# Complex products by three real ones, the overlap of one spectrum on VectorE, and a new order of stores and table transfers, in a long convolution with a gated state space model

## The chip, the cores and the metric

The kernel runs on one core of a Trainium2 chip. The metric is the device time of one execution in microseconds (us). The core's engines each work through a queue of their own in order and wait for one another by semaphores: TensorE (PE) multiplies matrices into PSUM, VectorE (DVE) and ScalarE (ACT) work elementwise, GpSimd (POOL) here mostly issues transfers that add into their destination, and SyncE (SP) issues the plain and the transposing transfers.

## What is computed

Two layers are mixed by a gate. Layer A is a diagonal state space model over 2048 steps with 1024 channels and 1024 complex states. Layer B multiplies a short convolution of k (4 taps) by v and convolves the product along the sequence with a filter as long as the sequence itself.

```python
g = sigmoid((x * gate_w).sum(-1, keepdims=True))
# layer A
B_bar = ((Lam_bar - 1.0) / Lam)[:, None] * Bmat
Bu = einsum("bld,pd->blp", x + 0j, B_bar)
for t in range(L):
    h = Lam_bar[None, :] * h + Bu[:, t, :]
y = 2.0 * einsum("blp,dp->bld", hseq, Cmat).real + x * Dskip
# layer B (q is x)
kv = k_shift * v
y = irfft2(rfft2(kv_pad) * rfft2(kf_pad))[:, :S]
y = x * (y + kv * ssm_D)
# out
g * a + (1 - g) * b
```

All inputs and the output are bfloat16; x, k and v have 2048 rows of 1024 columns.

## The kernel before, in words

**Layer B by blocks.** The 1024 channels are taken in eight groups of 128 (c = 0 to 7). The sequence is cut into four blocks of 512. Filter and signal of a block are folded and multiplied by cosine and sine tables on PE: `fwd_K` (line 636) forms the filter's spectrum in four tiles `psk`, `fwd_V` (line 674) the signal's in four tiles `psv`. ACT copies them from PSUM to `KH[c]` (kept in the buffers `BT` 2 and 3 by turns) and `VH[c]` (tiles `Vh`). Each holds two parts (c = 0 cosine, 1 sine), four blocks and 512 frequencies: 4096 columns.

The filter's block b overlaps block b - 1. For all groups but the last, `fwd_K` has PE add this part: eight more matmuls of 384 columns in each pair of tiles (lines 647 to 649). For group 7 DVE does it afterwards (`overlap_K`, line 667).

`products` (line 687) multiplies the spectra: a complex product for each pair of blocks (a, b) with a + b under 4, summed by the output block. It does so with four real products for a complex one. `A` in `acc` collects them; `wkh` and `t` hold parts. One addition of 3072 columns (from `n1`, in `wkh`) is not done by DVE but by an adding transfer that POOL issues (`gather`, line 717). The last four operations combine the parts and write the inverse's input back into `Vh` (`whole[c]`). `inverse` (line 769) multiplies it by inverse tables on PE (two tiles `psz`), ACT copies the tiles to `cv`, and SP stores them to scratch memory `cv_scr` (line 782).

Ahead of the spectra, `taps` (line 573) makes the short convolution on PE, `times_v` (line 603) multiplies by v on DVE and mirrors the result (`mirror` on PE, `lo` on ACT, `ev` on DVE, an adding transfer into `ks`). `fold_columns`, `fold_K` and `mirror_K` fold the filter. `spread` makes shifted copies of `kT` and `kB` for `taps`.

**Layer A in the gaps.** `Bu` (line 835) multiplies x by B in 16 pairs of tiles, odd and even rows apart. For the first two groups `Bu_tile` (line 867) runs in three steps: 16 matmuls into a tile `odd`, 16 into `even`, and four with a diagonal of lambda that close `even`. For the next two `Bu_halves` (line 892) has two such products of 16 and an empty step. `parts` (line 1187) is a generator over the 24 steps of these four; the main loop steps through it to put the products between the work of layer B. `turn_table` (line 471) builds a table of angles: ACT writes `hr`, a transfer adds its halves, and ACT takes sines in the next iteration.

**The order** is written by hand. `put` (line 93) makes each instruction follow the one before it on its engine, so an engine's queue is the order in which the Python code calls it; nearly every instruction therefore carries line 95 in the profile. The main loop (line 1190) runs c = 0 to 6. Iteration c runs the inverse of c - 1, the products of c, the spectra of c + 1 and the folding and taps of c + 2. All PSUM tiles come from one pool of four. After the loop come the products and inverse of group 7, the rest of Bu, the scans on DVE and the output product with C on PE (tiles `psy`).

## Time and profile before

| | |
|---|---|
| median of three runs | 382.45 us (378.86 to 383.15) |
| the profiled execution | 381.19 us, its span 379.4 us |
| granted TensorE clock | 0.998 of full speed |
| instructions in the span | 6680 |
| ACT busy | 303.6 us, 80% of the span |
| POOL busy | 78.0 us, 21% |
| bytes moved by transfers | 70.99 MB, mean 187 GB/s |
| `acc<-wkh`, 768 KB each, six times | median 8.3 us from issue to landing |
| `cv_scr<-cv`, 256 KB each, 16 times | median 3.7 us |
| `hr<-hr`, 256 KB each, four times | median 6.4 us |

A row of the timeline gives the start of an instruction or of several merged ones, their length, the engine, the operation with the tile it writes and the tiles it reads (out<-in), its shape, and a count. In square brackets stands how long the engine was idle ahead of it and who released it. In the answer on waits a row reads: engine and tile, who it waited for, microseconds in all, times, the longest. In the chain of work that ended last each row is a stretch of the path from the first to the last instruction, with the engine that held it. Matmuls overlap, and their ends are modelled: one of 512 columns is listed with 379 ns, while their starts are 216 ns apart.

### The profile page before, as it was taken

Reading aid. Unit: us, or ns where it says so; the run is one execution under the profiler, and the core shown is the slowest. Engines: PE = TensorE matmul, PEld = TensorE weight load, DVE = VectorE, ACT = ScalarE, POOL = GpSimd, SP = SyncE. Lnnn points to the kernel's source line nnn. Section 1 sums busy time; section 2 is a strip of 40 time slices with the busy share of each in tenths; the row PEclk is TensorE's granted clock in tenths of the full one; section 3 lists DMA queues with packets and bytes.
Section 4 is the critical chain, followed back from the end, with each engine's and each line's share of the span. In section 5 each row is a group of like instructions: output and inputs, shape, how many; then the busy total and the mean of one; then the engine's idle time right before and its main releaser. Section 6 shows DMA issues by size and latency. Waiting matters only on the chain.

```text
span 379.4 us, 6680 instructions
## 1 busy us (share of the span) xinstructions
PE 373.6 (98%) x2469; PEld 202.4 (53%) x2469; DVE 368.0 (97%) x596; ACT 303.6 (80%) x465; POOL 78.0 (21%) x106
## 2 busy tenths in 40 slices
PE   8999999999999999999999999999999999999996
PEld 5666457566584756754454444444445444444444
DVE  8899999999999999999999999999999999999984
ACT  5779998998989999777999699977979968936301
POOL 4011020020301102022012014122426322532000
PEclk9999999999999999999999999999999999999999
DMA  7879999999999998999999999946999998997223
GB/s 168 162 117 232 209 210 209 226 214 212 223 191 193 214 192 177 187 208 151 188 209 226 228 199 246 211 70 119 185 248 157 268 248 178 189 244 125 57 83 111
DMA packets 125827, 70.99 MB, mean 187 GB/s; under 512 B 104601, under 2 KB 107553, under 8 KB 125794
## 3 DMA queue, kind: packets, MB, share of 16 engines
q1 hardware_dynamic: 112416, 45.90, 55.4%
q0 software_dynamic: 12256, 24.38, 37.8%
q10 hardware_dynamic: 1122, 0.28, 0.4%
q8 instruction: 19, 0.31, 0.3%
q14 instruction: 14, 0.11, 0.1%
HBM read 15.48 MB, written 8.39 MB: 63 GB/s over the span
## 4 chain that ended last, share of the span: by engine, by line
PE 91%; DMA 6%; ACT 2%; SPq 0%; issue 0%; DVE 0%; ACTq 0%
PE psy L95 29%; PE both L95 22%; PE psk L95 10%; PE taps L95 6%; PE psv L95 6%; PE psz L95 5%; PE even L95 4%; PE odd L95 3%; DMA kT<-in_B_k_dram 3%; PE foldk L95 3%; DMA kT<-kT 2%; DMA kB<-kT 1%; ACT Vh L95 1%; PE p L95 1%; PE mirror L95 1%; ACT hr L95 1%
## 5 line engine op out<-in xcount | busy, mean ns | idle before, releaser
L95 PE MATMUL psy<-CT,U 128*128 128x512 bf16 (+1 forms) x426 | 93.2, 374 | 0.0
L95 PEld LDWEIGHTS <-U 128*128 128x128 bf16 x492 | 48.1, 98 | 55.6 <-issue 0.3
L95 PEld LDWEIGHTS <-BT 128*128 128x128 bf16 x544 | 50.5, 98 | 33.5 <-issue 0.2
L95 DVE TENSOR_TENSOR wkh<-BT,Vh 128x2048 bf16<-128x2048 bf16 (+3 forms) x31 | 44.7, 1460 | 0.0
L95 POOL DMA_DIRECT2D U<-Q x26 | 27.1, 1053 | 82.8 <-ACT Q L95 24.8
L95 DVE TENSOR_TENSOR acc<-BT,Vh 128x4096 bf16<-128x4096 bf16 (+3 forms) x19 | 37.0, 1950 | 0.6 <-ACT Vh L95 0.6
L95 ACT ACTIVATE Q<-U,lam 128x512 bf16<-128x512 bf16 (+1 forms) x60 | 35.0, 626 | 2.6 <-issue 1.9
L95 PE MATMUL both<-xT,BT 128*128 128x512 bf16 x160 | 35.3, 379 | 0.0
L95 ACT ACTIVATE Vh<-psv 128x1024 bf16<-128x1024 f32 x32 | 30.7, 1032 | 5.6 <-PE psv L95 5.6
L95 DVE TENSOR_TENSOR_SCAN A<-rv,init,A 128x256 bf16<-128x256 f32 x48 | 34.4, 736 | 0.0
L95 DVE TENSOR_TENSOR acc<-acc,wkh 128x1024 bf16<-128x1024 bf16 (+4 forms) x30 | 32.7, 1130 | 0.1
L95 ACT ACTIVATE BT<-psk 128x1024 bf16<-128x1024 f32 x31 | 30.1, 1037 | 2.3 <-PE psk L95 2.2
L95 ACT ACTIVATE U<-both 128x512 bf16<-128x512 f32 x44 | 24.3, 594 | 8.1 <-PE both L95 7.8
L95 POOL DMA_DIRECT2D acc<-wkh x8 | 9.8, 1219 | 100.2 <-DVE wkh L95 100.2
L95 PE MATMUL psk<-eok,SF 128*128 128x384 bf16 (+1 forms) x120 | 28.5, 354 | 0.0
L95 PEld LDWEIGHTS <-SF 128*128 128x128 bf16 x184 | 18.0, 98 | 18.8
L95 ACT ACTIVATE BT<-psy,gcols 128x1024 bf16<-128x1024 f32 (+1 forms) x6 | 6.3, 1043 | 24.7 <-issue 14.0
L95 PE MATMUL taps<-dg,kT 128*128 128x128 bf16 (+1 forms) x352 | 23.3, 219 | 1.0 <-DMA kT<-kT 0.5
L95 PE MATMUL psz<-Vh,CI 128*128 128x512 bf16 x64 | 24.3, 379 | 0.0
L95 PE MATMUL psz<-Vh,SI 128*128 128x512 bf16 x64 | 24.3, 379 | 0.0
L95 PEld LDWEIGHTS <-kT 128*128 128x128 bf16 x352 | 22.8, 104 | 2.7 <-DMA kT<-in_B_k_dram 1.4
L95 DVE TENSOR_TENSOR U<-U,trn 128x512 bf16<-128x512 bf16 (+1 forms) x60 | 22.0, 391 | 0.1
(225 smaller groups left out, 784.0 us busy)
## 6 DMA issues: line engine op xcount, KB each, us to landing
U<-Q POOLq DMA_DIRECT2D x26, 256.0 KB, 5.2
acc<-wkh POOLq DMA_DIRECT2D x6, 768.0 KB, 8.3
cv_scr<-cv SPq DMA_DIRECT2D x16, 256.0 KB, 3.7
kn<-in_B_ssm_k_dram SPq DMA_DIRECT2D x5, 512.0 KB, 4.4
v<-in_B_v_dram SPq DMA_DIRECT2D x5, 512.0 KB, 5.0
out_dram<-m SPq DMA_DIRECT2D x8, 256.0 KB, 4.6
BT<-cv_scr SPq DMA_DIRECT2D x7, 256.0 KB, 7.2
out_dram<-BT SPq DMA_DIRECT2D x7, 256.0 KB, 2.0
```

What stands on the lines that cost most here:

```text
L95: i = f(*a, **kw)
```

## The change

- Groups 1 to 7 get a `products` of their own with three real products for a complex one. DVE first forms the sum and the difference of the signal's two parts (`Vp`), and the sum of the filter's two parts (`S`, by the new `sum_K`); `pair` multiplies both filter parts by `Vp`, `one` multiplies `S` by the signal's first part. Group 0 keeps the old form as `products_0`.
- The adding transfer now adds both parts of `both` (3072 columns, as before), ahead of fewer operations of DVE. For group 7 DVE still does this addition itself.
- `apart_K = (3, NC - 1)`: spectrum 3 loses its overlap matmuls as spectrum 7 had done. `overlap_K` writes the overlapped blocks to a place in `wkh` (`K_later`) with two operations of 1536 columns.
- The steps of B are dealt out by a table, `count`; group (2, 0) runs its four products tile by tile, odd before even. There are 20 steps, since the empty ones are gone.
- For the inverses of c = 1 to 4, the stores of `cv` are issued only behind the load of v (`store_cv`).
- `turn_table`'s transfer is issued right after ACT's part, ahead of that of the products.
- `mirror_K` yields before its second copy, and with spectrum 3 the diagonals and the column fold for the next group come later in ACT's queue.

```diff
+    apart_K = (3, NC - 1)
+    K_later = {}
@@ mirror_K
         act(lo, ps, func=ACT.Copy)
+        yield
         act(eo[:, 1], kb[:, 2:4], func=ACT.Copy)
-        yield
@@ fwd_K
-                    mm(ps[:, cc], tab[:, mt, fsl], eo[:, cc, mt], mt == 0, c == NC - 1 and mt == 1)
-                for mt in range(0 if c == NC - 1 else 2):
+                    mm(ps[:, cc], tab[:, mt, fsl], eo[:, cc, mt], mt == 0, c in apart_K and mt == 1)
+                for mt in range(0 if c in apart_K else 2):
@@ overlap_K
-        for b in (3, 2, 1):
-            tt(K[:, 0, b], K[:, 0, b], K[:, 1, b - 1], ALU.add)
-            tt(K[:, 1, b], K[:, 1, b], K[:, 0, b - 1], ALU.subtract)
+        t = K_later[c] = WK[:, 4096:7168].rearrange("p (c b x) -> p c b x", c=2, b=3)
+        tt(t[:, 0], K[:, 0, 1:], K[:, 1, 0:3], ALU.add)
+        tt(t[:, 1], K[:, 1, 1:], K[:, 0, 0:3], ALU.subtract)
+
+    def sum_K(c):
+        S = sums[:, 1, 2048:].rearrange("p (b x) -> p b x", b=4)
+        if c in K_later:
+            tt(S[:, 0], K[:, 0, 0], K[:, 1, 0], ALU.add)
+            tt(S[:, 1:], K_later[c][:, 0], K_later[c][:, 1], ALU.add)
+        else:
+            tt(S, K[:, 0], K[:, 1], ALU.add)
@@ products, groups 1 to 7
+        def pair(o, b, n):
+            tt(o, bc(Kb(b), [128, 2, n, w]), Vp[:, :, 0:n], ALU.mult)
+        def one(o, b, n):
+            tt(o, bc(S[:, b:b + 1], [128, n, w]), V0[:, 0:n], ALU.mult)
+        tt(Vp[:, 1], Vt[:, 1], Vt[:, 0], ALU.add)
+        tt(Vp[:, 0], Vt[:, 1], Vt[:, 0], ALU.subtract)
+        yield
+        pair(both, 0, 4)
+        yield
+        pair(n1, 1, 3)
+        if by_dma:
+            gather(both[:, :, 1:], n1)
+        yield
...
+        pair(n3, 3, 1)
+        one(third, 0, 4)
+        yield
+        one(m1, 1, 3)
+        one(m3, 3, 1)
+        if not by_dma:
+            tt(both[:, :, 1:], both[:, :, 1:], n1, ALU.add)
+        one(m2, 2, 2)
+        tt(third[:, 1:], third[:, 1:], m1, ALU.add)
+        yield
+        pair(n2, 2, 2)
+        tt(m2[:, 1:], m2[:, 1:], m3, ALU.add)
+        tt(n2[:, :, 1:], n2[:, :, 1:], n3, ALU.add)
+        tt(third[:, 2:], third[:, 2:], m2, ALU.add)
+        yield
+        tt(both[:, :, 2:], both[:, :, 2:], n2, ALU.add)
+        yield
+        if c + 1 < NC and c + 1 not in apart_K:
+            sum_K(c + 1)
+        tt(both[:, 1], third, both[:, 1], ALU.subtract)
+        tt(both[:, 0], third, both[:, 0], ALU.add)
+        if c + 1 in apart_K:
+            sum_K(c + 1)
...
         tt(to[:, 0], lo, hi, ALU.subtract)
         tt(to[:, 1], lo, hi, ALU.add)
@@ inverse
-            move(cv_scr[c, :, 2 * par:2 * par + 2], cv)
+            stores.append((cv_scr[c, :, 2 * par:2 * par + 2], cv))
+            if c == 0 or c >= 5:
+                store_cv()
@@ main
-    parts = (None for i in range(4) for b in Bu(i) for _ in b)
+    def in_parts():
+        for i in range(4):
+            for b in ([tile_ for pair_ in [Bu(2)] for _ in range(2) for tile_ in pair_] if i == 2 else Bu(i)):
+                for _ in range(1 if i == 2 else 3 if i < 2 else 2):
+                    step(b)
+                    yield
+    count = {1: "D1 F1 G2", 2: "A1 B1 C1 D1 E2 F1", 3: "D2 F1", 4: "C1 D1 F1", 5: "D1 F2"}
...
+        if c == 1:
+            sum_K(1)
         step(old)
-        step(tabs)
+        steps(tabs, 2)
         run(back)
         step(tv)
-        steps(prod, 4)
+        steps(prod, 3)
...
             elif c < 5:
                 load("v", nn, True)
+                store_cv()
+            at("D")
             taps(nn, dg)
+            at("E")
             if c == 5:
                 load("v", nn)
+                store_cv()
...
         run(fk)
+        step(prod)
+        if n in apart_K:
+            overlap_K(n)
         run(prod)
-        if n == NC - 1:
-            overlap_K(n)
```

The letters of `count` are places in an iteration: A ahead of the first two tiles of `fwd_K`, B between its halves, C behind it, D ahead of `taps`, E behind it, F behind the first step of `times_v`, G between the halves of `fwd_V`; the number is how many steps run there. Before, the steps stood at D and F in nearly every iteration, at G in c = 1 and 3, and at other places in c = 2, 4, 5 and 6.

156 lines of the change are left out of this document (78 added, 78 removed).

## The prediction

> **What bounds the kernel now.** I read the page first: which engine is full, and what carries the chain that ended last.
>
> ```profile
> span 379.4 us, 6680 instructions
> PE 373.6 (98%) x2469; PEld 202.4 (53%) x2469; DVE 368.0 (97%) x596; ACT 303.6 (80%) x465; POOL 78.0 (21%) x106
> PE 91%; DMA 6%; ACT 2%; SPq 0%; issue 0%; DVE 0%; ACTq 0%
> ```
>
> TensorE (PE) is busy 98% of the span and VectorE (DVE) 97%. A busy PE need not run at its peak, so I asked next for PE's waits and then for the chain in order of time.
>
> ```profile
> PE taps L95 <- DMA kT<-kT: 0.5, 1, 0.5
> PE taps L95 <- DMA kT<-in_B_k_dram: 0.5, 1, 0.5
> ```
> ```profile
> 86.72 1.75 PE even L95 x16
> ...
> 142.31 6.05 PE psk L95 x32
> ...
> 165.25 3.45 PE psk L95 x16
> ```
>
> These are all of PE's waits after its first microsecond. The chain's rows (start, length, engine, tile, count) give PE's prices: one product of B, 16 matmuls, takes 1.75 us; a spectrum of K with its 16 overlap matmuls takes 6.05 us, the last one, which has none, 3.45. PE's starts follow each other at this pace from 59.5 us to the end, so PE's queue sets the time. DVE has hardly an idle stretch either: what it delivers to PE comes just in time, and any microsecond added to it can turn into a wait of PE. I judge the change by both: how much work leaves PE, and where PE then reaches something that another engine hasn't finished.
>
> **PE's work.** Spectrum 3 loses its 16 overlap matmuls: 6.05 - 3.45 = **2.60 us off**. The products of B are only moved. Counting the steps, whole products (odd or even) per iteration c = 1 to 6 go from 3, 3, 3, 3, 3, 1 to 3, 5, 2, 3, 3, 0. So PE's clock against before is +2 x 1.75 - 2.60 = +0.90 us at the end of c = 2, then -1.75 more in c = 3 and -1.75 in what lies ahead of the inverse of c = 5.
>
> **DVE's work**, from the timeline of one product stage (c = 4), and two other places for short operations:
>
> ```profile
> 116.86 2.29 DVE L95 TENSOR_TENSOR acc<-BT,Vh 128x4096 bf16<-128x4096 bf16 x1 [0.34 <-ACT Vh L95]
> 119.07 1.75 DVE L95 TENSOR_TENSOR wkh<-BT,Vh 128x3072 bf16<-128x3072 bf16 x1
> 120.73 2.29 DVE L95 TENSOR_TENSOR acc<-BT,Vh 128x4096 bf16<-128x4096 bf16 x1
> ...
> 124.61 0.69 DVE L95 TENSOR_TENSOR ev<-ks,lo 128x1024 bf16<-128x1024 bf16 x1
> 125.21 1.75 DVE L95 TENSOR_TENSOR acc<-acc,wkh 128x3072 bf16<-128x3072 bf16 x1
> ...
> 128.01 2.35 DVE L95 TENSOR_TENSOR wkh<-BT,Vh 128x2048 bf16<-128x2048 bf16 x2
> 130.28 1.29 DVE L95 TENSOR_TENSOR wkh<-wkh,t 128x1024 bf16<-128x1024 bf16 x2
> ...
> 133.83 2.35 DVE L95 TENSOR_TENSOR acc<-acc 128x2048 bf16<-128x2048 bf16 x2
> 136.21 2.36 DVE L95 TENSOR_TENSOR Vh<-acc 128x2048 bf16<-128x2048 bf16 x2
> ```
> ```profile
> 32.55 0.95 DVE L95 TENSOR_TENSOR wkh<-BT,Vh 128x1536 bf16<-128x1536 bf16 x1
> 33.42 0.69 DVE L95 TENSOR_TENSOR acc<-acc,t 128x1024 bf16<-128x1024 bf16 x1
> ```
> ```profile
> 185.68 2.35 DVE L95 TENSOR_TENSOR BT<-BT 128x512 bf16<-128x512 bf16 x6
> 187.94 4.42 DVE L95 TENSOR_TENSOR acc<-BT,Vh 128x8192 bf16<-128x8192 bf16 x1
> ```
>
> Neighbours overlap, so I price from start to start: 4096 elements 2.21 us, 3072 1.66, 2048 1.135 (half of 2.27), 1536 0.87, 1024 0.60, 512 about 0.38 (2.26 over six). An operation that needs the result of the one straight before it adds 0.11 (133.83 to 136.21 is 2.38 for a pair, not 2.27).
>
> The old stage takes 116.86 to 136.21 = 19.35 us up to the inverse's input `Vh`. The new one has eight of 2048 (9.08), one of 4096 (2.21), one of 3072 (1.66), two of 1536 (1.74), five of 1024 (3.00, `ev` among them), two of 512 (0.76) and three such neighbours (0.33): 18.78. So three real products are worth only 0.57 us a stage: fewer elements, but 21 operations for 18. The Trainium skill ("VectorE: DVE Perf Modes", section "The DRAIN you can't avoid") speaks against this shape: the pipe empties after every operation, so their number should be kept small. The rows' own price of one more operation is 2 x 1.135 - 2.21 = 0.06 us, and it is in the sum already.
>
> Around it: c = 1 forms its own K sum first (+1.135, net +0.57). c = 2 takes on the overlap of spectrum 3 (two of 1536, 1.74) and splits its sum (+0.1): net +1.27. c = 6 has the same ahead of its `Vh` (+1.27), where six operations (2.26) stood behind it. c = 7 saves about 1.7, since it adds 3072 elements where it added 6144, and forms no further sum. In all DVE saves some 2.8 us, but is late by 0.57 + 1.27 = 1.84 us at the end of c = 2. From c = 7 on it is ahead, so the scans cost PE nothing.
>
> **Where PE waits instead.** First a held PSUM tile. The last `even` tile of group (1, 1) now opens at the end of c = 2 and is closed in c = 3, so iteration 3 starts with three rotating PSUM tiles, not four. PE's first spectrum tile must wait for ScalarE's (ACT's) first `cv`; before, it was the second.
>
> ```profile
> 96.08 0.59 PE L95 MATMUL psk<-eok,CF 128*128 128x512 bf16 x2
> ...
> 97.27 0.49 PE L95 MATMUL psk<-eok,NCF 128*128 128x384 bf16 x2
> 97.82 0.59 PE L95 MATMUL psk<-eok,CF 128*128 128x512 bf16 x2
> ```
> ```profile
> 93.48 0.66 ACT L95 ACTIVATE hr<-hr 128x512 f32<-128x512 f32 x1
> ...
> 96.73 1.95 ACT L95 ACTIVATE cv<-psz 128x1024 bf16<-128x1024 f32 x2
> ...
> 135.88 3.77 ACT L95 ACTIVATE Vh<-psv 128x1024 bf16<-128x1024 f32 x4 [0.27 <-PE psv L95]
> ```
>
> Before, PE lost only 0.23 us here (97.27 to 97.82 for two matmuls of 0.16). Now PE comes to that point at 96.08 + 0.90 = 96.98. ACT empties four `Vh` tiles in a row (as at 135.88), which moves its table work from 93.48 to about 94.35 and frees the first `cv` at 97.82 + 0.87 = 98.69. That is a wait of 1.71, **1.48 more** than before. Its bounds are -0.23 (ACT early) and 1.71. PE's clock after c = 3 is then +0.90 + 1.48 - 1.75 = +0.63.
>
> Second, DVE against the inverse of c = 5 and c = 6, and of c = 1:
>
> ```profile
> 66.46 2.36 DVE L95 TENSOR_TENSOR Vh<-acc 128x2048 bf16<-128x2048 bf16 x2
> ...
> 159.64 2.36 DVE L95 TENSOR_TENSOR Vh<-acc 128x2048 bf16<-128x2048 bf16 x2
> ...
> 183.41 2.36 DVE L95 TENSOR_TENSOR Vh<-acc 128x2048 bf16<-128x2048 bf16 x2
> ```
> ```profile
> 68.76 0.38 PE L95 MATMUL psz<-Vh,CI 128*128 128x512 bf16 x1
> ...
> 161.21 0.38 PE L95 MATMUL psz<-Vh,CI 128*128 128x512 bf16 x1
> ...
> 186.61 0.38 PE L95 MATMUL psz<-Vh,CI 128*128 128x512 bf16 x1
> ```
>
> The first half of `Vh` is done 1.22 us after its start, at 160.86 for c = 5. The stage starts when ACT has emptied PE's `psv`, so with PE: 160.86 + 0.63 - 0.57 = 160.92. PE now wants it at 161.21 + 0.63 - 1.75 = 160.09. **PE waits 0.83.** From 0 (DVE quicker by that much) to 1.5 if the bubbles between short operations are twice mine. At c = 6 `Vh` is ready at 184.63 + 0.06 + 1.27 = 185.96, PE comes at 186.61 - 0.29 = 186.32: no wait.
>
> At c = 1 PE lost 0.73 us waiting for `kT<-kT` (0.5 of it in the row above; the rest is the modelled end of its last matmul). The table's transfer now goes before the large gather, and the gather itself starts later, so `kT<-kT` has less beside it. But `Vh` of c = 1 is ready at 66.46 + 1.22 + 0.57 = 68.25 where PE would come at 68.76 - 0.73 = 68.03: at most 0.51 is won, at least 0. I take **0.4 off**, since only a small wait for the gather stands against it.
>
> The gather is the unknown:
>
> ```profile
> 49.31 1.75 DVE L95 TENSOR_TENSOR wkh<-BT,Vh 128x3072 bf16<-128x3072 bf16 x1
> ```
> ```profile
> 51.36 1.20 POOL L95 DMA_DIRECT2D acc<-wkh  x1 [14.69 <-DVE wkh L95]
> ```
> ```profile
> acc<-wkh POOLq DMA_DIRECT2D x1, 768.0 KB, 9.4
> ```
> ```profile
> acc<-wkh POOLq DMA_DIRECT2D x1, 768.0 KB, 6.5
> ```
> ```profile
> DMA to landing us min/median/max: 6.1/8.0/9.4
> ```
>
> GpSimd (POOL) issues it 2.05 us after the start of DVE's operation that fills `n1`. From `ev` to the operation that needs it lie 7.8 us of DVE work by the prices above, after the 1.66 of `n1`: DVE is there 7.4 us after the issue, where by the same prices it used to come 11.5 us after it. The same transfer took 9.4 us beside two stores of `cv` and a `kT<-kT` (c = 2), and 6.5 in c = 6, where the stores were over sooner. Moving those stores behind `v`, some 10 us later, empties its neighbourhood in c = 2 to 5, so I take 7.4 or less: no wait. The stores themselves sit in SyncE's (SP's) queue ahead of the `kT` load, which is held for ACT anyway, so they cost nothing there unless they slow `v`. The Trainium skill ("DMA: Bandwidth & Descriptors", section "Anatomy of one DMA — SWDGE (gpsimd) path") gives 2.0 us plus bytes over 436 GB/s, an estimate of 3.8 us here. By that the gather never matters and the sum stays as it is; the rows above stand at 6.5 to 9.4, so the trace disagrees and the rows decide.
>
> The remaining edits are free: `mirror_K`'s copy moves behind ACT's other work in c = 5, and its result is used ten microseconds later (PE's 165.25). The later fold of spectrum 4 leaves ACT's queue for the earlier K tiles.
>
> **The sum.** -2.60 + 1.48 + 0.83 - 0.40 = -0.69 us. The profiled execution took 381.19 us with 1.8 around its span, and the runs shown have a median of 382.45 (378.86 to 383.15). From 381.19 I get **380.5 us**.
>
> **Rivals.** (1) PE's floor: ACT and DVE are early enough, so the held tile and the inverses cost nothing and both old waits go: 381.19 - 2.60 - 0.73 - 0.23 = **377.6**. For it: each wait I add is under 2 us and hangs on differences of a few tenths. Against it: both come from work that is counted, not guessed. (2) The gather lands late, the mechanism that ends slower: if it keeps its old landing times, 9.4 where I quoted it and near 8 to 9.4 elsewhere, c = 1 to 5 lose about 1.9, 2.0, 0.5, 0.7 and 1.1, in all 6.2 us on DVE. `Vh` of c = 5 comes at 160.86 + 0.57 + 1.27 - 3 x 0.57 - 0.34 (the wait on ACT that it swallows) + 6.2 = 166.85, PE's inverse starts 5.6 us later than before, and nothing gives that back: **386.8**. It decides from landings of about 7.5 us on: 0.7 us in all of such waits uses up the gain. For it: nearly all landings of before lie above that. Against it: the neighbours that made them long are moved. (3) The deferred stores meet `v` and `kT` on the DMA queues, and `taps` of the next iteration waits as at 59.5 us, 0.5 to 0.7 in three iterations: about **382**.
>
> **Numbers.** My forecast 0.45, (1) 0.28, (2) 0.19, (3) 0.08. About 1% is what a measurement of this kernel can tell from no change. The range runs from 377.2, just under (1), to 384.8, which holds a half-late gather; what lies beyond is the upper half of (2) and little else. Faster by over 1% takes a time under about 377.5 to 378.6, depending on which of the runs is the base: most of (1), 0.24. Slower by over 1%: the larger part of (2), 0.17. Within 1%: 0.59.
>
> **What would show it.** PE's chain should show spectrum 3 at 3.45 us. A gap of PE before the first `psk` near 97 to 99 us, released by ACT's `cv`, confirms the held tile; its absence speaks for (1). A PE gap before `psz` near 160 us, released by DVE, confirms the second. DVE's busy time should come out near 365 us. A DVE wait on `acc`'s DMA ahead of the last addition, repeated in c = 1 to 5, would make me wrong toward (2), and landings of `acc` say by how much. If `taps` waits for `kT` or `kB` in several iterations, it is (3).

## The result, and the profile after

The changed kernel is slower: 385.49 us in the median of 20 runs (382.61 to 398.0) against 380.17 for the kernel before (378.86 to 392.48, also 20). The ratio is 1.0111 with an interval of 1.0075 to 1.0146; like all ratios below it is formed without the executions that are several us slower at a lower clock. The forecast was 380.5, with a range up to 384.8. Each kernel has one profile, of a single execution. The experiments are read mainly from where things stand in these profiles, and the ratios are beside them.

The page of the changed kernel (span, busy time of the engines, and the chain that ended last by engine):

```profile
span 380.8 us, 6658 instructions
PE 370.1 (97%) x2453; PEld 199.4 (52%) x2453; DVE 365.3 (96%) x620; ACT 303.5 (80%) x465; POOL 76.6 (20%) x106
PE 78%; issue 10%; DMA 6%; DVE 2%; ACT 2%; POOL 1%; POOLq 0%; DVEq 0%; ACTq 0%
```

PE and DVE both do less than before (373.6 and 368.0), and yet the span is longer. So something waits. The answer on PE's waits (us in all, times, the longest) has four rows after the start:

```profile
PE psv L95 <- DMA ks<-lo: 2.4, 1, 2.4
PE psk L95 <- ACT cv L95: 1.5, 1, 1.5
...
PE odd L95 <- DMA xT<-in_A_x_dram: 1.1, 1, 1.1
PE psz L95 <- DVE Vh L95: 0.7, 1, 0.7
```

The second and the fourth were forecast (1.71 and 0.83). The first and the third were not. To place them, here are PE's rows from the timeline: the first inverse matmul of c = 0, c = 1 and c = 6 (`psz`), and the four waits.

```profile
43.18 0.39 PE L95 MATMUL psz<-Vh,CI 128*128 128x512 bf16 x1
...
56.50 1.91 PE L95 MATMUL odd<-xT,BT 128*128 128x256 bf16 x16 [1.14 <-DMA xT<-in_A_x_dram]
...
64.90 0.59 PE L95 MATMUL psv<-ks,SF 128*128 128x512 bf16 x2 [2.44 <-DMA ks<-lo]
...
70.10 0.38 PE L95 MATMUL psz<-Vh,CI 128*128 128x512 bf16 x1
...
99.99 0.59 PE L95 MATMUL psk<-eok,CF 128*128 128x512 bf16 x2 [1.52 <-ACT cv L95]
...
162.51 0.39 PE L95 MATMUL psz<-Vh,CI 128*128 128x512 bf16 x1 [0.69 <-DVE Vh L95]
...
187.93 0.38 PE L95 MATMUL psz<-Vh,CI 128*128 128x512 bf16 x1
```

The same mark for c = 0 in the kernel before (those of c = 1 and c = 6, 68.76 and 186.61, stand in the prediction), and the first `psv` that reads `ks` there, which doesn't wait:

```profile
45.00 0.39 PE L95 MATMUL psz<-Vh,CI 128*128 128x512 bf16 x1
...
63.55 0.59 PE L95 MATMUL psv<-ks,SF 128*128 128x512 bf16 x2
```

These marks cut the comparison into stretches that don't depend on the start, which was 1.82 us quicker in this execution of the changed kernel (43.18 for 45.00) although the code up to there is nearly the same, and varied between 43.1 and 45.9 over all the kernels below.

| from psz to psz | before | after | difference |
|---|---|---|---|
| c = 0 to c = 1 | 23.76 | 26.92 | **+3.16** |
| c = 1 to c = 6 | 117.85 | 117.83 | -0.02 |

Behind the mark of c = 6 the two spans differ by nothing: 379.4 - 186.61 = 192.8 and 380.8 - 187.93 = 192.9. **In these two profiles all of the loss lies in iteration 1.**

That last stretch is not always so short. Of the 19 profiles of this document ten have 192.7 to 194.3 us there and nine 196.5 to 206.3, among them the kernel before with one edit (experiment 4). In all nine PE waits 2.5 to 2.8 us for ACT's `U` ahead of a `psy`, and ACT has waited 4.3 to 13.5 us for loads between 225 and 262 us; in the ten others ACT waits 2.5 or less. In the last kernel of the table below (timelines of ACT and of PE):

```profile
243.51 1.15 ACT L95 ACTIVATE pbb<-pbb,omg 128x1024 bf16<-128x1024 bf16 x1 [5.57 <-DMA pbb<-cv_scr]
```
```profile
256.87 1.02 PE L95 MATMUL psy<-CTa,U 128*128 128x512 bf16 x4 [2.83 <-ACT U L95]
```

So a profiled time can be some 4 us or more longer for a reason that lies behind the loop. How often this happens to each kernel is not known, with one profile of each.

In iteration 1 POOL issues in another order. Before, and after (timeline of POOL):

```profile
55.84 0.91 POOL L95 DMA_DIRECT2D ks<-lo  x1 [3.28 <-DVE ev L95]
56.41 1.22 POOL L95 DMA_DIRECT2D hr<-hr  x1
```
```profile
46.20 0.89 POOL L95 DMA_DIRECT2D hr<-hr  x1 [11.35 <-ACT hr L95]
53.07 1.21 POOL L95 DMA_DIRECT2D acc<-wkh  x1 [5.99 <-DVE wkh L95]
53.78 1.43 POOL L95 DMA_DIRECT2D ks<-lo  x1
```

The transfers of iteration 1 and their landing in us, in the changed kernel:

```profile
hr<-hr POOLq DMA_DIRECT2D x1, 256.0 KB, 9.2
```
```profile
acc<-wkh POOLq DMA_DIRECT2D x1, 768.0 KB, 9.2
```
```profile
ks<-lo POOLq DMA_DIRECT2D x1, 256.0 KB, 11.1
```

Before, the gather left at 51.36 and `ks` 4.5 us behind it; `ks` landed in 7.1, at 62.9, just ahead of the `psv` that reads it, at 63.55. Now `hr` leaves first, the gather later, and `ks` 0.7 us behind the gather. It lands at 53.78 + 11.1 = 64.9, and that is where PE goes on. `xT` is late too: SP's issue of its transposing load took 3.08 us before and takes 4.15 beside `hr`.

```profile
48.74 3.08 SPq L95 DMA_TRANSPOSE xT<-in_A_x_dram  x1
```
```profile
46.15 4.15 SPq L95 DMA_TRANSPOSE xT<-in_A_x_dram  x1
```

### The profile page after: what moved, and what is told of

The parts are those of the page before. It is cut to its first block, busy times and chain, and to the rows that moved or that the text cites. A ratio compares the mean times of both kernels' runs of the same rounds, so it can differ in the third digit from the quotient of the medians.

```text
span 380.8 us, 6658 instructions
## 1 busy us (share of the span) xinstructions
PE 370.1 (97%) x2453; PEld 199.4 (52%) x2453; DVE 365.3 (96%) x620; ACT 303.5 (80%) x465; POOL 76.6 (20%) x106
## 4 chain that ended last, share of the span: by engine, by line
PE 78%; issue 10%; DMA 6%; DVE 2%; ACT 2%; POOL 1%; POOLq 0%; DVEq 0%; ACTq 0%
PE psy L95 29%; PE both L95 22%; PE psk L95 8%; PE psz L95 5%; PE psv L95 4%; PE taps L95 4%; DMA acc<-wkh 3%; DMA ks<-lo 3%; PE foldk L95 2%; PE even L95 2%; PE odd L95 1%; DVE acc L95 1%; PE p L95 1%; ACT Vh L95 1%; PE mirror L95 1%
## 5 line engine op out<-in xcount | busy, mean ns | idle before, releaser
L95 DVE TENSOR_TENSOR acc<-acc,Vh 128x2048 bf16<-128x2048 bf16 (+2 forms) x28 | 26.6, 951 | 1.8 <-DMA acc<-wkh 1.8
L95 PEld LDWEIGHTS <-SF 128*128 128x128 bf16 x176 | 17.2, 98 | 20.9 <-issue 2.7
L95 PE MATMUL psk<-eok,SF 128*128 128x512 bf16 (+1 forms) x112 | 27.2, 356 | 0.0
L95 PEld LDWEIGHTS <-kT 128*128 128x128 bf16 x352 | 21.6, 101 | 1.3 <-DMA kT<-in_B_k_dram 0.8
L95 PE MATMUL taps<-dg,kT 128*128 128x128 bf16 (+1 forms) x352 | 22.0, 212 | 0.0
L95 PE MATMUL psv<-ks,SF 128*128 128x512 bf16 x64 | 19.0, 379 | 2.4 <-DMA ks<-lo 2.4
L95 PE MATMUL both<-xT,BTl 128*128 128x512 bf16 x96 | 21.2, 379 | 0.0
L95 PE MATMUL both<-BT,BT 128*128 128x512 bf16 x96 | 21.0, 379 | 0.0
```

The lines of the kernel that those rows point to most:

```text
L95: i = f(*a, **kw)
```

## The experiments

Two theories stood at the start. A: DVE forms S and Vp first, so the gather leaves later, and `ks` queues behind it. B: the table's transfer, issued first, slows the others. Beside these, the two waits that were forecast had to be tested, and rival (2)'s reason. Each edit is against the changed kernel unless it says otherwise. The table collects the readings: landing of the three transfers of iteration 1 from their issue, PE's longest wait there, and the two stretches between marks. "Half" marks a stretch in which PE's granted clock fell to half for some 3.4 us.

| kernel | acc | ks | hr | PE's longest wait in c = 1 | psz 0 to 1 | psz 1 to 6 |
|---|---|---|---|---|---|---|
| before | 9.3 | 7.1 | 8.9 | taps 0.55 | 23.76 | 117.85 |
| after | 9.2 | 11.1 | 9.2 | psv 2.44 | 26.92 | 117.83 |
| ks first in c = 1 | 10.6 | 4.2 | 6.8 | psz 3.47 | 27.08 | 119.33 half |
| table in its old place | 6.5 | 7.3 | 10.3 | psv 0.24 | 23.25 | 118.82 |
| no held tile | 7.9 | 11.2 | 6.1 | psv 4.04 | 28.67 half | 117.73 |
| stores at once | 7.4 | 10.2 | 5.6 | psv 3.05 | 27.69 half | 117.63 |
| old place in c = 1 alone | 6.4 | 7.3 | 10.3 | psv 0.19 | 23.25 | 119.75 |
| before, with table first | 7.8 | 6.8 | 5.5 | odd 1.28 | 24.53 | 118.04 |
| first stores deferred | 6.4 | 9.3 | 5.6 | psv 2.20 | 26.82 half | 117.62 |
| old place, no held tile | 6.5 | 7.3 | 10.2 | psv 0.23 | 23.26 | 118.60 |
| xT ahead | 8.9 | 10.4 | 5.3 | taps 2.12 | 26.95 half | 117.85 |
| four remedies | 6.5 | 7.3 | 10.2 | psv 0.19 | 23.24 | 118.56 |
| table behind lo | 8.0 | 10.7 | 5.6 | psv 2.83 | 28.19 half | 117.62 |
| B's load behind taps | 7.9 | 9.9 | 6.1 | psv 2.77 | 27.17 half | 117.64 |
| ks ahead everywhere | 8.3 | 5.6 | 10.8 | psz 1.67 | 24.83 | 120.32 |
| plain store first | 7.6 | 8.3 | 10.4 | psv 0.99 | 24.17 | 118.52 |
| three remedies | 6.5 | 7.3 | 10.7 | none listed | 23.26 | 118.53 |
| a transfer behind ks | 8.9 | 10.4 | 6.6 | psv 3.06 | 26.23 | 117.63 |

**1. ks first.** In c = 1, `ev` and the `ks` transfer come ahead of `pair(n1)` and its gather.

```diff
-        steps(prod, 3)
+        steps(prod, 2 if c == 1 else 3)
         run(tv)
+        if c == 1:
+            step(prod)
```

> Only in c = 1, times_v's adding transfer into ks and DVE's ev come ahead of pair(n1) and its gather; all else as in the changed kernel. Theory A (the changed kernel loses in c = 1 because DVE forms S and Vp first, so the 768 KB gather leaves 3.6 us later and the 256 KB ks transfer queues behind it): ks then leaves at about 52.1 us instead of 53.8, lands near 59 to 60, and PE's first psv (61.9) doesn't wait; the 2.4 us row goes. The gather leaves 0.6 us later, so DVE still waits for it about 1.8 us and Vh of c = 1 moves from 68.3 to about 68.9, where PE would come at 67.7: psz waits about 1.2. Net 1.0 to 1.5 us quicker than the changed kernel. Theory B (the table's transfer, issued ahead of both at 46.2, is what makes these transfers slow): ks still lands after 63 us, psv still waits 1 to 2.4, and the time moves by less than 0.7.

Measured: 386.53 us in the median, 1.0164 (1.0092 to 1.0235). `ks` landed in 4.2 and `psv` didn't wait. But the gather took 10.6, so DVE waited for it (timeline of DVE) and PE for DVE (timeline of PE):

```profile
64.39 1.23 DVE L95 TENSOR_TENSOR acc<-acc,Vh 128x2048 bf16<-128x2048 bf16 x1 [3.73 <-DMA acc<-wkh]
```
```profile
70.33 0.39 PE L95 MATMUL psz<-Vh,CI 128*128 128x512 bf16 x1 [3.47 <-DVE Vh L95]
```

Theory A was half right: ahead of the gather `ks` is not late. But taking it there didn't help, since the gather itself was slow. Theory B was half wrong too: it had `ks` landing after 63 us, and it landed at 56.3. The order of these two alone is not what costs the time.

**2. The table's transfer in its old place**, in every iteration:

```diff
-        steps(tabs, 2)
+        step(tabs)
         run(back)
         step(tv)
         steps(prod, 3)
         run(tv)
+        step(old)
+        step(tabs)
         run(old)
```

> The table's transfer goes back to its old place behind the gather and ks in every iteration, the rest as in the changed kernel. Theory B (table's transfer first slows what stands beside and behind it): in c = 1 xT lands sooner and PE's 1.1 us wait of odd goes, the gather lands in 8 us or less instead of 9.2 and ks in 8 to 9 instead of 11.1, psv waits under 0.7; the time falls by 2 to 3.5 us. Theory A (the late gather with ks behind it): psv's wait for ks stays at 2 or more, and kT<-kT or xT still takes some tenths; the time is within 1 us of the changed kernel.

Measured: 380.72 us, 1.0003 (0.9957 to 1.0048): the loss is gone, within that interval. In the profile the mark of c = 1 (timeline of PE, with that of c = 0) stands 23.25 us behind c = 0, which is 0.51 less than before the change.

```profile
43.87 0.39 PE L95 MATMUL psz<-Vh,CI 128*128 128x512 bf16 x1
...
61.86 0.59 PE L95 MATMUL psv<-ks,SF 128*128 128x512 bf16 x2 [0.24 <-DMA ks<-lo]
...
67.12 0.39 PE L95 MATMUL psz<-Vh,CI 128*128 128x512 bf16 x1
...
78.42 1.05 PE L95 MATMUL odd<-xT,BT 128*128 128x256 bf16 x8 [0.72 <-DMA BT<-in_A_B_im_dram]
```

The landings, in the order of issue:

```profile
acc<-wkh POOLq DMA_DIRECT2D x1, 768.0 KB, 6.5
```
```profile
ks<-lo POOLq DMA_DIRECT2D x1, 256.0 KB, 7.3
```
```profile
hr<-hr POOLq DMA_DIRECT2D x1, 256.0 KB, 10.3
```

`ks` still stands 0.7 us behind the gather, and yet lands in 7.3. Now `hr` is the slow one, and nobody waits for it before the next iteration. Theory B holds: the transfer's place causes the loss. Of the 3.67 won up to the mark of c = 1 some comes back at once: PE reaches the first product of group 1 so early that it waits for B, 0.72 us at 78.42. The products that the change brought forward to c = 2 had found B ready only because PE was late. From c = 0 to c = 6 this kernel takes 142.07 us, 2.68 less than the changed kernel and 0.46 more than the one before. The profiled execution took 384.96 us all the same, since it is one of the nine with a long stretch behind the mark of c = 6 (197.3).

How far can one profile be trusted? Five more kernels below have the same order of POOL's transfers in iteration 1 and no added store, and all give 23.24 to 23.26 for c = 0 to c = 1. Two others ("no held tile" and "stores at once") have the changed kernel's iteration 1 and give 28.67 and 27.69 for its 26.92, with the gather landing in 7.9 and 7.4 for its 9.2 and `ks` in 11.2 and 10.2 for its 11.1. So the loss repeats, but its parts vary by up to 1.8 us from one execution to the next.

**3. In c = 1 alone.** The old place in c = 1, first from c = 2 on (the same lines with `if c == 1`).

> The table's transfer is in its old place (behind the gather and ks) in c = 1 alone, and first from c = 2 on. Theory B1 (it does harm only in c = 1, where it starts beside xT's transposing load): as with the old place everywhere, 380.0 to 381.0 us, in c = 1 no wait of odd for xT over 0.3, the gather in 6.5 to 7.5 us, ks in 7 to 8.5. Rival (it costs something in c = 2 to 5 too): 381.5 us or more, with waits there that the run with the old place everywhere doesn't show.

Measured: 1.0057 (1.0006 to 1.0109); the median of 388.38 comes from widely scattered runs (380.77 to 398.43). In the profile iteration 1 is the same as in experiment 2 to the hundredth (23.25), so the 3.67 us are lost in c = 1. But the wait for B in c = 2 is longer, 1.95 us at 78.96: B's load lands 8.5 us behind the start of its issue (70.49), against 7.3 in experiment 2, and here the table's transfer leaves right beside it, at 71.13. The stretch from c = 1 to c = 6 is 119.75 for 118.82. That is what the rival expected, a cost from c = 2 on as well, about 0.9 us once PE is no longer late; one profile is little to show it by, and the two intervals overlap.

**4. The kernel before, with the table's transfer first.** One part of the change by itself:

```diff
         step(old)
-        step(tabs)
+        steps(tabs, 2)
...
         run(tv)
         step(old)
-        step(tabs)
         run(old)
```

> The kernel before with one part of the change alone: the table's transfer issued right behind ACT's part. Theory B (the early transfer slows xT's load and what SP issues behind it): xT's issue takes 4 to 6 us on SP instead of 3.1, kT<-kT leaves 1 to 3 us later, and taps or odd of c = 1 waits 1.5 to 3 us instead of 0.5; 1.5 to 3 us slower than before. Rival (it hurts only together with the change's late gather and the ks transfer straight behind it): within 0.6 us of before, since ks leaves 4.5 us behind the gather here.

Measured: 1.0037 (0.9987 to 1.0087). `xT`'s issue took 5.12 us, `odd` waited 1.28, and the mark of c = 1 moved by 24.53 - 23.76 = 0.77. Between the two forecasts: the early transfer costs something by itself, but less than a quarter of the 3.67 it costs beside the new products, where `ks` leaves straight behind the gather and has no 4.5 us to spare.

**5. The stores of cv.** Twice: issued at once everywhere (as before the change), and the opposite, with those of c = 0 deferred as well.

```diff
-            if c == 0 or c >= 5:
-                store_cv()
+            store_cv()
```

> The stores of cv are issued at once in every iteration, as in the kernel before; the rest as in the changed kernel. Theory S (the stores beside the gather made its landing long, and moving them behind v saved the change from rival 2): acc lands in 8 to 9.4 us in c = 2, 3 and 5 instead of 6.4, DVE waits for it 0.5 to 2 us in each, psz waits longer, and the time rises by 2 to 6 us. Rival (the landing is set by the gather itself or by the order on its own queue): acc stays at 6.3 to 7.2 us, DVE waits only in c = 1, and the time stays within 0.5 us.

```diff
-            if c == 0 or c >= 5:
+            if c >= 5:
                 store_cv()
...
                 load_BT(1, 0, True)
+                store_cv()
```

> The changed kernel with the two cv stores of the inverse of c = 0 deferred too, behind the load of B in c = 1; the table's transfer stays first. Theory B2 (the early transfer holds up xT's issue on SP, and so puts kT<-kT and the two stores beside the gather, which is what makes it land late): without the stores the gather of c = 1 lands in 7.5 us or less instead of 9.2 and ks in 8.5 or less instead of 11.1, psv waits under 0.7, xT's 1.1 stays; 1.5 to 2.4 us quicker than the changed kernel. Rival (the gather is slow because of xT's load itself or the table's transfer, not because of the stores): ks at 10 or more, psv waits 1.5 or more, time within 0.7 us of the changed kernel.

Measured, at once: 1.0112 (1.0066 to 1.0157), no change. The gather landed in 6.9, 6.8, 7.6 and 6.4 us in c = 2 to 5, and DVE waited for it 0.2 in all. The deferring was not what kept rival (2) away. In the kernel before, the stores were issued within 0.2 us of the gather in these iterations (75.27 against 75.10 in c = 2) and it took 7.9 to 9.4; with the new products it leaves 0.9 to 2.5 us behind them even when they are not deferred, because Vp comes first. The store that is closest, 0.9 us, goes with the 7.6.

Measured, deferred in c = 0 too: 1.0108 (1.0073 to 1.0144), also no change, but not for want of an effect. The gather fell from 9.2 to 6.4 and `ks` from 11.1 to 9.3. PE came earlier and waited 2.20 us all the same, and then its clock halved. The rows are the timeline of PE, and the busy time in stretches of 2 us (PE, PEld, DVE, ACT, POOL, then the granted clock, the DMA share and GB/s):

```profile
63.28 0.59 PE L95 MATMUL psv<-ks,SF 128*128 128x512 bf16 x2 [2.20 <-DMA ks<-lo]
```
```profile
64.00:66.00 2.00, 2.00 (x11) 1.24 (x10) 1.97 (x3) 2.00 (x3) 0.00 (x0) 0.65 1.06 328
66.00:68.00 2.00, 2.00 (x12) 1.42 (x10) 2.00 (x3) 0.34 (x1) 0.00 (x0) 0.50 1.47 286
```

That is 0.35 x 2 + 0.50 x 2 = 1.7 us of PE's work lost, about what the earlier landing (63.3 for 64.9) had won. Beside the other profiles of the changed kernel's iteration 1 (gather 7.4 to 9.2, `ks` 10.2 to 11.2) the stores account for 1.0 to 2.8 us of the gather's landing and 0.9 to 1.9 of that of `ks`. They carry a part of the loss, then, not all.

**6. xT, its neighbours, and B's load.** Three guesses at what the early transfer disturbs. First, `xT`'s load moved ahead of the spread of `kT`:

```diff
+            load_xT(0, (1,))
             apart = spread(3)
             step(apart)
-            load_xT(0, (1,))
             run(apart)
```

> The changed kernel with one move on SP: at the end of c = 0 xT's transposing load is issued ahead of the spread of kT (kB<-kT, kT<-kT), so that it starts some 2 us sooner and is nearly issued when the table's transfer, which stays first, begins. Theory B3 (the harm comes from the table's transfer starting together with xT's load, whose issue it stretches from 3.1 to 4 to 6 us, and from all that follows on SP): xT's issue takes 3.5 us or less, odd doesn't wait for it, ks of c = 1 lands in 8.5 us or less, psv waits under 0.7, kT<-kT may add 0.5 at taps; 2 to 3 us quicker than the changed kernel, 380.0 to 381.5. Rival (on its own queue the table's transfer holds up the gather and ks, wherever xT stands): ks at 9 to 11, psv waits 1.5 or more, time within 1 us of the changed kernel.

Then, ACT's filling of `hr` behind `lo` in c = 1, so that the transfer leaves at 51.26, behind `xT`'s issue but ahead of the gather:

```diff
-        steps(tabs, 2)
+        if c > 1:
+            steps(tabs, 2)
         run(back)
         step(tv)
+        if c == 1:
+            steps(tabs, 2)
```

> The changed kernel with one move in c = 1: ACT fills hr behind the two cv and lo, not ahead of them, so the table's transfer leaves near 50.5 to 51 us instead of 46.2, behind xT's issue on SP (which ends at 50.1 when undisturbed) but still ahead of the gather and ks on POOL's queue. The cv stores leave some 1.8 us sooner. Theory B4 (what hurts is that the table's transfer runs while SP issues xT's transposing load): xT's issue takes 3.0 to 3.3 us, kT<-kT leaves near 50, the gather lands in 7.5 us or less and ks in 8.5 or less, odd and taps don't wait, psv waits under 1; psz of c = 1 starts 23.2 to 24 us behind psz of c = 0 instead of 26.9, and the time is 2.5 to 3.5 us under the changed kernel's. Rival (its place ahead of the gather and ks on POOL's queue is what hurts): ks at 9.5 us or more, psv waits 1.5 or more, psz 25.5 us or more behind psz of c = 0.

And the load of B in c = 1 behind `taps`:

```diff
-            if c == 1:
-                load_BT(1, 0, True)
-            elif c < 5:
+            if 1 < c < 5:
                 load("v", nn, True)
...
             taps(nn, dg)
+            if c == 1:
+                load_BT(1, 0, True)
```

> The changed kernel with one move in c = 1: the transposing load of B (first half of group 1) is issued behind taps instead of ahead of it, so SP issues it near 61.4 us instead of 58.0; the table's transfer stays first. Theory C (whichever transfer stands last in POOL's queue in c = 1 is dragged out, to 63 to 65 us in all runs so far, by SP's issue of this load from 58 us on; with the table's transfer in its old place that one is last and shields ks): ks lands by 62 us, 8.5 us or less behind its issue, psv waits 0.5 or less for it, and psz of c = 1 starts 23.3 to 24.8 us behind psz of c = 0 instead of 26.9; some of it is lost again, since both halves of B arrive 2 to 3 us later and odd of c = 2 waits for them 1 to 4 us. Rival D (the drag has nothing to do with that load): ks still lands at 63 us or later, psv waits 1.5 or more.

Measured: 1.0266 (1.0202 to 1.0330), 1.0108 (1.0068 to 1.0148) and 1.0062 (1.0016 to 1.0108). All three guesses fell, the first in part. With `xT` ahead its issue was short (2.03) and `odd` no longer waited, but `kT<-kT` left at 53.77, 3.4 us later than in the changed kernel, `taps` waited 2.12 for it, and `ks` still took 10.4. With the transfer moved behind it, `xT`'s issue was undisturbed (3.02) and `kT<-kT` left at 51.19, but the gather took 8.0 and `ks` 10.7. With B's load moved from 58.0 to 60.4, `ks` took 9.9. With the new products and `ks` behind the gather, whenever the table's 256 KB go first in c = 1, `ks` lands 9.3 us or more behind its issue in every profile, whatever SP has beside it. In six of these eight profiles the table's transfer had landed before the gather left (experiment 5, deferred: 46.34 + 5.6 = 51.9, and 53.20). So it need not be under way beside them to do its harm. One of the ten executions with B's load moved took 379.45 us, as little as the kernel before, while the profiled one took 387.23; whether `ks` is late in every execution of that kernel is not shown.

**7. The same bytes, elsewhere.** On the kernel of experiment 2, a plain store of 256 KB on SP's queue right ahead of `xT`'s load, of a table into a part of `cv_scr` that is written again later:

```diff
+            move(cv_scr[NC - 1, :, 0:2], CF.rearrange("p a (b d) -> p a b d", d=128))
             load_xT(0, (1,))
```

> The kernel with the table's transfer in its old place, and a plain 256 KB store added on SP's queue right ahead of xT's load at the end of c = 0 (from a table to a part of cv_scr that is written again much later), as large as the table's transfer and at the same time, but not on POOL's queue and without adding. Theory E (the DMA engines are full from 46 to 64 us, so 256 KB more ahead of xT, the gather and ks pushes them all back): xT's issue ends 1 to 2 us later, the gather lands in 7.5 to 9 us and ks in 8.5 to 10 instead of 6.5 and 7.3, psv waits 1 to 2.5, and psz of c = 1 starts 24.2 to 26 us behind psz of c = 0 instead of 23.25. Rival F (it is the adding transfer on POOL's own queue that matters, not the bytes): ks stays at 8 us or less, psv waits under 0.6, psz at 24 or less.

And on the changed kernel, a further adding transfer of 256 KB behind `ks`, onto a half of `hr` that is overwritten before it is read (`hrs[0]` holds that half and the other one):

```diff
         run(tv)
+        if c == 1:
+            gather(*hrs[0])
```

> The changed kernel with one transfer added in c = 1, behind ks on POOL's queue: as large as the table's (256 KB, adding), onto a half of hr that is overwritten before anything reads it. Everything ahead of ks stays as in the changed kernel. Theory G (in c = 1 whatever stands last on POOL's queue is dragged out; the table's transfer in its old place only shielded ks): ks lands in 8.5 us or less instead of 11.1, the added transfer takes 10 or more, psv waits under 1, psz of c = 1 starts 24.0 to 25.5 us behind psz of c = 0 instead of 26.9. Rival (it is what goes ahead of ks that delays it: the early transfer's bytes, xT and the stores pushed back): ks still at 9.5 or more, psv waits 1.8 or more, psz at 26 or more.

Measured with the plain store: 1.0033 (0.9996 to 1.0070); timeline of SP and of PE:

```profile
47.07 4.18 SPq L95 DMA_TRANSPOSE xT<-in_A_x_dram  x1
```
```profile
62.08 0.59 PE L95 MATMUL psv<-ks,SF 128*128 128x512 bf16 x2 [0.99 <-DMA ks<-lo]
```

`xT`'s issue is stretched as in the changed kernel (4.18, from 3.05), the gather goes from 6.5 to 7.6, `ks` from 7.3 to 8.3, and the mark of c = 1 by 0.92. That lies between the two expectations: a plain store as large does about a quarter of the harm (0.92 of 3.67). The Trainium skill ("DMA: Bandwidth & Descriptors", section "Queues, rings and completion order") has each DMA engine take turns between the queues. That fits a store on SP's queue delaying a transfer on POOL's by 1.1 us, but no run here shows the turns. The added store also pushed the two stores of `cv` closer to the gather: they left 1.0 us ahead of it instead of 2.9, and with stores 0.9 us ahead the gather took 7.6 in experiment 5 too.

Measured with the added transfer: 389.67 us in four runs. `ks` was no longer last and still took 10.4, the added one 11.4:

```profile
66.50 0.59 PE L95 MATMUL psv<-ks,SF 128*128 128x512 bf16 x2 [3.06 <-DMA ks<-lo]
```

So it isn't its place at the end of the queue that makes `ks` late, as the landing of `hr` in experiment 2 had suggested. It is what goes ahead of it.

**8. The held tile.** The last `even` of group (1, 1) is dealt from c = 2 to c = 3, on the changed kernel and on that of experiment 2:

```diff
-    count = {1: "D1 F1 G2", 2: "A1 B1 C1 D1 E2 F1", 3: "D2 F1", 4: "C1 D1 F1", 5: "D1 F2"}
+    count = {1: "D1 F1 G2", 2: "A1 B1 C1 D1 E2", 3: "D1 F2 G1", 4: "C1 D1 F1", 5: "D1 F2"}
```

> The last even product of group (1,1) is dealt from the end of c = 2 to c = 3, so that no PSUM tile stays open over the start of iteration 3; one product of B moves with it. Theory H (the held tile makes psk of c = 3 wait for ACT's first cv): the 1.5 us row psk <- ACT cv goes to 0.3 or less; PE comes to psz of c = 2 1.75 us sooner, at 92.7, where Vh is ready at 93.1, so 0.4 comes back; 0.9 to 1.3 us quicker. Rival: ACT is late at this place whatever the number of tiles; then psk or a later tile of c = 3 waits 1 us or more all the same and the time stays within 0.4 us.

> The changed kernel with the table's transfer in its old place everywhere and without the held tile (one product dealt from c = 2 to c = 3). Theory H: psk <- ACT cv goes from 1.5 to 0.3 or less, psz of c = 2 waits 0.4 for DVE instead; 1 us quicker than with the old place alone, 379.3 to 380.0 us. Rival: ACT is late at that place anyway; 380.3 us or more, with a wait of 1 us or more at psk in c = 3.

Measured: 1.0102 (1.0033 to 1.0171) and 1.0032 (0.9979 to 1.0086). The row of `psk` for `cv`, 1.5 in every other kernel with this order of products, is gone in both, so the held tile makes that wait. But the time is not won: on the second kernel `psz` of c = 2 waits 1.28 for DVE's `Vh` in its place, and the stretch to c = 6 is 118.60 for 118.82.

**9. Spectrum 3 on PE again**, on the kernel of experiment 2 (`apart_K = (NC - 1,)`).

> The kernel with the table's transfer in its old place, with spectrum 3 overlapped by PE again (16 more matmuls, no overlap or split sum on DVE in c = 2). If PE's queue sets the time as the prediction says, PE has 2.6 us more in c = 2, the 0.7 us wait of odd for BT is swallowed, the held tile's 1.5 stays: 1.7 to 2.6 us slower than the old-place kernel, 381.8 to 382.8. Rival (DVE sets it, so work given back to PE costs nothing): within 0.5 us of the old-place kernel, 380.0 to 381.0.

Measured: 1.0081 (1.0058 to 1.0105). The stretch from c = 1 to c = 6 grows from 118.82 to 120.23, by 1.41 us: PE's 2.60 is worth about half on the end. The executions' times speak for the first expectation (the quickest took 381.32 us, 1.68 more than the quickest of experiment 2), the stretch for something less than its 1.7 to 2.6. So PE's queue does set the time, and DVE, given less to do, returns some of it.

**10. All remedies together.** The old place; the overlap and sum of K for groups 3 and 7 behind DVE's `Vh`; the products of c = 2, 3 and 5 dealt anew:

```diff
-    count = {1: "D1 F1 G2", 2: "A1 B1 C1 D1 E2 F1", 3: "D2 F1", 4: "C1 D1 F1", 5: "D1 F2"}
+    count = {1: "D1 F1 G2", 2: "A1 B1 D2 E2", 3: "D1 E1 F1 G1", 4: "C1 D1 F1", 5: "D1 F1"}
...
+        if c == 6:
+            step(parts)
         run(back)
...
-        step(prod)
-        if n in apart_K:
-            overlap_K(n)
         run(prod)
+        if n in apart_K:
+            overlap_K(n)
+            sum_K(n)
```

> Four remedies together on the changed kernel: the table's transfer in its old place; DVE's overlap and sum of K for groups 3 and 7 behind the operations that write Vh of the group before; one product of B from c = 2 to c = 3 with no held tile, and the first product of group 1 behind the folds of c = 2; one product from c = 5 back ahead of the inverse of c = 5. If each wait is what its row says (psk 1.5, odd for BT 0.7, psz of c = 2 up to 1.3 and of c = 5 0.7), PE has no wait over 0.4 after c = 1 until the tail, and the time is the old-place kernel's less 2.2 to 2.9: 377.3 to 378.5 us, quicker than before by 0.2 to 0.6%. Rival (DVE, busy 96% of the span, is the bound, and a wait taken away comes back as one on DVE or ACT further on): 379.5 to 380.7 us, with new waits of psz or psy of 1 us or more.

Then the same with `ks` ahead of the gather everywhere, and with overlap and sum behind the product of k and v:

> As the kernel with four remedies, and further: in every iteration ev and the ks transfer come ahead of pair(n1) and its gather, and the overlap and sum of K for groups 3 and 7 stand behind the product of k and v. If the waits of that kernel (psv for ks 2.0 in three places, mirror for ks 0.6) are what took the 2.6 us of PE back, ks lands in 4 to 5 us everywhere, psv never waits, and psz of c = 6 comes 139.5 to 140.7 us behind psz of c = 0 (before: 141.6; four remedies: 141.8): 377.3 to 378.3 us for an undisturbed execution. Rival (DVE carries the loop: what PE gains it waits for elsewhere): 141.2 or more, with DVE waiting for the gather or PE for Vh by 1 us or more in several iterations.

And at last with `ks` behind the gather again and c = 5 as in the changed kernel:

> The kernel with four remedies, with two of its flaws taken out: the products of c = 5 stay as in the changed kernel (0.7 us for DVE's Vh in place of 1.3 for ks), and the overlap and sum of K for groups 3 and 7 stand behind the product of k and v (mirror no longer waits 0.6). If waits add up: psz of c = 6 comes 140.2 to 141.1 us behind psz of c = 0 (before 141.6, four remedies 141.8), 378.0 to 378.8 us when undisturbed. Rival (DVE carries the loop, every wait cured comes back): 141.5 or more.

Measured: 1.0041 (1.0005 to 1.0078), 1.0051 (1.0007 to 1.0096) and 1.0010 (0.9985 to 1.0036). None beats the kernel before. Each wait that a row had named is gone (no `psk` for `cv`, no `odd` for B, and in the first no `psz` for `Vh`), and others are there: in the first `psv` for `ks` 2.0 in three places and `mirror` for DVE's `ks` 0.6; in the second `psz` for `Vh` 4.7; in the third `psv` for `ks` 1.8. The third one's busy time from the mark of c = 1 to that of c = 2, and on to that of c = 3, shows why:

```profile
66.89:90.01 23.12, 22.77 (x206) 15.35 (x205) 22.98 (x29) 21.27 (x35) 3.13 (x4) 1.00 1.04 204
90.01:115.25 25.24, 23.45 (x201) 14.98 (x200) 25.14 (x28) 21.41 (x35) 3.13 (x4) 1.00 1.02 193
```

DVE is busy 25.14 of the 25.24 us, PE 23.45. The rivals of these three expectations hold in the main: in this stretch DVE carries the loop, and what leaves PE with spectrum 3 has gone to it. The first rival named `psz` or `psy` for the new waits, and it was `psv`, with 1.26 at the most.

## Why the prediction was wrong

The step that failed is the term for iteration 1, "0.4 off, since only a small wait for the gather stands against it". It measured +3.16 (23.76 to 26.92), 3.56 us more than that. PE's two new waits in the stretch are for `ks` (2.44) and for `xT` (1.14). The sentence took the early table's transfer as a relief ("so `kT<-kT` has less beside it") and priced no wait for `ks` at all. Three things were missed, readable from the rows of before and the order of the new code. `ks` was to leave right behind a 768 KB gather, not 4.5 us later, with 0.6 us to spare before `psv` (landing at 62.9, read at 63.55); it is the transfer on POOL's queue that no sentence of the prediction names. The table's transfer would start beside `xT`'s load: before, ACT had filled `hr` at 47.7, and `xT` was issued from 48.74. And the stores of c = 0 weren't deferred: the prediction has the gather's neighbourhood emptied in c = 2 to 5, as it was, and allows for c = 1 only "a small wait for the gather", where it landed in 9.2 and DVE waited 1.8 for it.

The term does not explain the whole miss. The forecast was added to a profiled execution with a start 1.82 us longer; the profile after took 382.61 us, and the median of 385.49 lies 2.9 above that, for reasons that no profile of the changed kernel shows.

With the table's transfer in its old place the same stretch came out at -0.51, close to the -0.40. The gain was there, then, but not from the part of its reason that named the table's transfer: PE had no wait for `kT<-kT` without it too. That leaves why the early transfer harms. Shown: its place in c = 1 brings or takes the whole 3.67 us; it is what goes ahead of `ks`, not the end of the queue; a plain store as large does a quarter of it; without the two stores beside the gather `ks` is still late, at 9.3. What makes an adding transfer worse than a plain store there, and how the remaining parts share out, stays open.

The other steps, in their order:

- **Spectrum 3 without overlap**: right. The chain in order of time shows its two halves with 1.73 each, 3.46 together:

```profile
75.89 1.73 PE psk L95 x8
78.06 1.73 PE psk L95 x8
```

- **The held tile**: 1.71 was forecast, 1.52 measured, released by ACT's `cv` as told; taking the tile away took the wait away.
- **`psz` of c = 5 for DVE**: 0.83 forecast, 0.69 measured.
- **DVE's stage**: from `Vp` to `Vh` in c = 4 it was priced at 18.78, and measures 137.60 - 118.86 = 18.74:

```profile
118.86 2.36 DVE L95 TENSOR_TENSOR wkh<-Vh 128x2048 bf16<-128x2048 bf16 x2 [0.78 <-ACT Vh L95]
...
137.60 2.36 DVE L95 TENSOR_TENSOR Vh<-acc 128x2048 bf16<-128x2048 bf16 x2
```

  DVE's total of "near 365" is 365.3.
- **The gather**: 7.4 or less was assumed, and it lands in 6.4 to 6.5 from c = 2 to 6 without a wait. The assumption was right, its reason only in part: the stores at once gave 6.4 to 7.6, so most of the gain seems to come from the gather itself leaving later, behind the stores.
- **The sum from c = 1 to c = 6**: -2.60 + 1.48 + 0.83 = -0.29 was forecast, -0.02 measured. That it came so near is partly luck: PE was late from c = 1, and this hid other waits. With the table's transfer in its old place the same stretch takes 118.82, +0.97 instead of -0.29. The waits that this uncovers, for B (0.7 to 2.0) and for DVE, weren't in the sum.
- **Behind the loop**: no effect was forecast, none found (192.8 and 192.9).
- **Rivals**: (1), the floor, didn't come, and the three attempts of experiment 10 to cure the waits didn't reach it. (2) named the late gather, and the only late one was that of c = 1 (DVE waited 1.8 us for it); but its price reached PE through `ks`, not through `Vh`, and the four later iterations stayed free. (3) didn't come: no `taps` waited.

So the forecast of a time near that of before describes the change without its early table transfer (1.0003), not the change as it was made.

## What to carry to other kernels

When a transfer is moved ahead on a queue, list every transfer behind it with the moment its reader needs it, and begin with the one that has the least to spare; a landing that was just in time is the first to be lost, even where the mover's own reader gains. Two engines at 97% bound each other: here 2.6 us taken from the first and given to the second were worth 1.4 in the stretch from c = 1 to c = 6, and the kernels with the waits cured were still no quicker than before. And where a change seems to cost one thing, undo its parts one by one before explaining it: here one line, which issues a transfer earlier, was the loss, within what these runs can tell.

## What the runs showed of the hardware

A wait of PE can cost more than its length. Nine profiles have a wait of PE of 2.1 us or longer up to the mark of c = 1 (2.12 to 4.04). In seven of them the granted clock fell to 0.50 for some 3.4 us, beginning between 0.5 us before the end of the wait and 1.4 us behind it, which takes 1.7 us more; the two without are the changed kernel's (2.44) and the one with a transfer behind `ks` (3.06). Later in the kernels it is alike: of eleven more waits of 2.1 us or longer (nine of 2.5 to 2.8 for `psy`, one of 4.5, one of 3.0) seven have such a fall beside them and four have none. None is near a wait of 1.95 us or less. The Trainium skill ("TensorE: Matmul & The Clock Gate", section "HAM oscillation — how this bites in real kernels") asks for no idle gaps of PE over about 3.4 us, behind which the clock is halved; the half clock agrees with these rows, but gaps of 2.1 us were enough here. With the loads that are late behind the loop, it is a likely part of why the changed kernel's median lies further from before (5.3 us) than its profile does, though that is argued, not shown.

In c = 2 to 5 an adding transfer of 768 KB landed in 6.4 to 6.5 us with no store close to it (the changed kernel), in 6.4 to 6.9 with two stores of 256 KB issued 2.0 to 2.5 us ahead, in 7.6 with 0.9, and in 7.9 to 9.4 with the stores issued beside it (the kernel before). The stores are not all: in experiment 2, without them and with the table's transfer straight behind, it took 6.4 to 7.2 there.
